# A recurrence and a mixture of experts in one kernel: TensorE's products of a step in another order

## The chip, the cores and the metric

The kernel runs on one core of a Trainium2 chip. The metric is the time of one execution on the device, in microseconds (us); the median of several runs counts. The profile comes from one more execution of the same kernel.

## The reference

```python
def _attn_ref(r, k, v, w, u):                       # B, H, S, D = 4, 8, 768, 48
    for t in range(S):
        kt, vt, rt = (k[:, :, t], v[:, :, t], r[:, :, t])
        cur = np.einsum('bhd,bhe->bhde', u[None] * kt, vt)
        y[:, :, t] = np.einsum('bhd,bhde->bhe', rt, state + cur)
        state = w[None, :, :, None] * state + np.einsum('bhd,bhe->bhde', kt, vt)
    return y

def _moe_ref(x, w_skip, w_gate, w1, w2):            # 3072 tokens of 384, 8 experts, F = 1024
    do_compute = x @ w_skip > 0
    xc = x[do_compute]
    logits = xc @ w_gate
    e_idx = np.argmax(logits, axis=1)
    gate_w = softmax(logits)[np.arange(len(xc)), e_idx]
    for e in range(E):
        h = np.maximum(xc[mask] @ w1[e], 0.0)       # mask: e_idx == e
        y[mask] = gate_w[mask, None] * (h @ w2[e])
    out[do_compute] = xc + y
```

The output of the recurrence, with the heads side by side, is the x of the experts.

## The kernel before

The recurrence is cut into chunks of 64 positions. One step handles one chunk of two batches and all heads; there are 24 steps (n = 0 to 23), 12 for each pair of batches. What a step puts on TensorE, by the function that does it:

- `scores(n+1)` (L496): products of the decayed r and k of the next chunk, 48 rows by 64 columns of the array each, four side by side, into `ps_p`. VectorE then writes them under a causal mask and on the diagonal into `am` (`mask_scores`, L508 and L509).
- `within(n)` (L550), the masked products: `am` of this chunk times v, all 128 rows by 64 columns, into `ps_y`.
- `turn_x(n-1)` (L619) and `turn_k(n+1)` (L482), the turns: transposes of the last chunk's output and of the next chunk's k, the whole array. ScalarE copies the results to `x4` (L623) and `kt` (L484).
- `state(n)` (L520), the state products: `kt` times v, 128 rows by 48 columns, added into `ps_s`. In three steps of four ScalarE then copies the state to `sblk` (`keep_state`, L538); in every fourth (n = 3, 7, 15, 19) VectorE first scales it in place (L531) and the copy comes after `across`.
- `across(n)` (L566), the carried products: r times the state in `sblk`, 48 rows by 64 columns, added onto the masked products in `ps_y`. ScalarE copies the sum out (`xt`, L579).

The last step of a pair of batches (n = 11, 23) has no state products, the first (n = 0, 12) no carried ones, and there is nothing to turn for k at n = 10 and 22.

The experts' choice runs beside this. After every fourth step `gate_four` (L636) computes the logits of four chunks, 128 rows by 32 columns, into `ps_t`; ScalarE copies them (L645), and `gate_back` (L650) turns them back. `route`, a generator, does the choice for groups of 8, 8, 4 and 4 chunks in small VectorE instructions; each `tick` or `step_route(kind)` in the loop lets it go on to its next yield of that kind. In it, `tri` and `ones` products count ranks (L732 to L742), and the list products (L841, L804) write which token goes where.

Everything is recorded by hand in the order of the code: each engine executes its instructions in that order, and waits only on semaphores of what it reads or overwrites. `behind(mm, name)` adds such a wait by hand: the first carried product waits for `turned_x[n-1]`, ScalarE's copy of the turn (L575). Products of the first expert fill the last two steps and what follows; the experts' loop comes after.

Each engine's instructions that precede VectorE's scaling in a step matter too: `prep_r(n+3)` (L446) on VectorE, after which ScalarE and GpSimd make the bonus part (L464, L456), the two mask instructions, and one tick of `route`.

## Time and profile before

| | |
|---|---|
| median of 3 runs | 271.28 us (269.43 to 272.10) |
| profiled execution, its own time | 266.43 us |
| its span, first to last instruction | 264.6 us |
| TensorE busy | 251.7 us (95%) |
| VectorE, ScalarE, GpSimd busy | 170.6, 139.4, 110.8 us |
| granted TensorE clock, mean | 0.994 |

The profiled execution was 1.8% shorter than the median of the runs, and its time is 1.8 us more than its span. The recurrence takes the first 113 us of the span, the experts the rest. TensorE's busy share says little by itself, since the ends of its matmuls are modelled; where the text needs the length of a stage it takes the distance between the starts of two stages.

### The profile page before, as it was taken

To read this page: it belongs to the slowest core of one execution; us is meant where nothing else is said; L and a number is where in the kernel's file an instruction comes from. 1 tells how busy PE (TensorE), PEld (TensorE's weight loads), DVE (VectorE), ACT (ScalarE), POOL (GpSimd) and SP (SyncE) were. 2 spreads that over 40 slices of the span, in tenths; PEclk is the share of its full clock that TensorE was granted. 3 is DMA by queue.
4 is the path that set the end of the run, shared out by engine and by line. 5 is a ranking of instruction groups with operands and counts; after the bars stand their busy time and mean duration, and the time that the engine had idled before them with its cause. 6 is when DMAs were issued, how large, how long until landed. Compare 5 with 4: busy or idle time off the path is not lost.

```text
span 264.6 us, 8597 instructions
## 1 busy us (share of the span) xinstructions
PE 251.7 (95%) x3579; PEld 225.5 (85%) x3581; DVE 170.6 (64%) x382; ACT 139.4 (53%) x315; POOL 110.8 (42%) x128
## 2 busy tenths in 40 slices
PE   7799998989999999999999999999999999999990
PEld 2578887778888888877789999999999999999990
DVE  7768555568664877737865967948659477494300
ACT  2566565656766756444773916637258174491200
POOL 8579554474765655501778151220310403105011
PEclk9999999999999999999999999999999999999997
DMA  6998699988997888496399979185291670101000
GB/s 159 245 254 257 196 257 245 274 216 242 254 265 215 246 250 266 103 345 203 108 305 285 330 215 386 54 296 231 57 398 60 223 301 18 30 0 35 11 32 24
DMA packets 20864, 52.21 MB, mean 197 GB/s; under 512 B 3556, under 2 KB 10224, under 8 KB 20816
## 3 DMA queue, kind: packets, MB, share of 16 engines
q1 hardware_dynamic: 18240, 46.42, 58.2%
q0 software_dynamic: 2048, 5.14, 6.2%
q8 instruction: 30, 0.49, 0.8%
q14 instruction: 18, 0.15, 0.2%
q10 hardware_dynamic: 528, 0.02, 0.1%
HBM read 43.77 MB, written 8.36 MB: 197 GB/s over the span
## 4 chain that ended last, share of the span: by engine, by line
PE 85%; DMA 7%; DVE 2%; issue 1%; ACT 1%; SPq 1%; POOL 0%; POOLq 0%; DVEq 0%
PE ps_p L178 11%; PE ps_y L178 11%; PE ps_l L168 11%; PE ps_p L496 8%; PE ps_y L550 7%; PE ps_s L520 6%; PE ps_p L168 5%; PE ps_x L168 5%; PE ps_y L566 5%; DMA dm<-in_dm_dram 4%; PE ps_t L619 4%; PE ps_l L482 3%; DMA raw<-in_w_dram 2%; PE ps_t L636 2%; PE ps_y L233 2%
## 5 line engine op out<-in xcount | busy, mean ns | idle before, releaser
L187 POOL DMA_INDIRECT out_dram<-xg,sid x16 | 23.7, 1478 | 89.8 <-DVE xg L183 79.8
L129 DVE TENSOR_TENSOR wlo<-raw,whi 128x512 fp32r<-128x512 f32 x84 | 54.0, 685 | 2.1 <-ACT whi L124 2.0
L124 ACT CAST whi<-raw 128x512 fp32r<-128x512 f32 x96 | 54.7, 626 | 0.0
L446 DVE TENSOR_TENSOR rd<-dm,w_d 112x512 f32<-112x512 f32 x24 | 17.7, 740 | 17.9 <-PE ps_y L566 15.6
L168 PE MATMUL ps_l<-x,whi 128*128 128x232 f32 x168 | 28.9, 274 | 0.0
L469 POOL TENSOR_TENSOR kd<-dm,w_d 112x512 f32<-112x512 f32 x22 | 28.1, 1278 | 1.0 <-DVE rd L446 1.0
L496 PE MATMUL ps_p<-rd,kd 48*64 48x128 f32 x768 | 26.4, 273 | 1.5 <-issue 0.8
L138 POOL DMA_INDIRECT xg<-out_dram,gid x16 | 19.3, 1204 | 19.7 <-DMA raw<-in_w_dram 13.4
L456 POOL TENSOR_TENSOR rd<-rd,uw 112x256 f32<-112x256 f32 x21 | 12.9, 615 | 33.1 <-DVE rd L446 23.3
L168 PEld LDWEIGHTS ps_l<-x,whi 128*128 128x128 f32 x168 | 25.5, 192 | 0.0
L464 ACT ACTIVATE rd<-rd,uw 112x128 f32<-112x128 f32 x52 | 18.0, 396 | 11.2 <-DVE rd L446 10.8
L496 PEld LDWEIGHTS ps_p<-rd,kd 48*64 48x64 f32 x768 | 20.9, 133 | 3.3 <-issue 1.4
L168 PE MATMUL ps_l<-x,wlo 128*128 128x232 f32 x84 | 23.2, 276 | 0.0
L172 ACT ACTIVATE hh<-ps_p 128x464 fp32r<-128x464 f32 x7 | 3.9, 559 | 33.1 <-PE ps_p L168 33.1
L550 PE MATMUL ps_y<-vkv,am 128*64 128x96 f32 x384 | 21.1, 252 | 0.1
L508 DVE COPY_PREDICATED am<-below,ps_p 128x512 f32<-128x512 int8 x24 | 17.7, 736 | 4.7 <-PE ps_p L496 4.3
L550 PEld LDWEIGHTS ps_y<-vkv,am 128*64 128x64 f32 x384 | 16.6, 136 | 4.2 <-issue 2.9
L520 PE MATMUL ps_s<-vkv,kt 128*48 128x96 f32 x352 | 19.4, 251 | 0.8 <-issue 0.8
L623 ACT COPY x<-ps_t 128x384 f32<-128x384 f32 x23 | 11.0, 478 | 16.0 <-PE ps_t L619 15.9
L178 PE MATMUL ps_p<-whi,hh 128*128 128x384 f32 x56 | 19.4, 347 | 0.0
L178 PE MATMUL ps_y<-whi,hh 128*104 128x384 f32 x56 | 18.9, 338 | 0.0
L178 PE MATMUL ps_p<-whi,hl 128*128 128x384 f32 x56 | 18.9, 337 | 0.0
(239 smaller groups left out, 591.2 us busy)
## 6 DMA issues: line engine op xcount, KB each, us to landing
raw<-in_w_dram SPq DMA_DIRECT2D x16, 768.0 KB, 7.9
dm<-in_dm_dram SPq DMA_DIRECT2D x24, 448.0 KB, 5.3
raw<-in_w_dram SPq DMA_DIRECT2D x24, 256.0 KB, 5.5
raw<-in_w_dram SPq DMA_DIRECT2D x12, 512.0 KB, 5.5
out_dram<-xt SPq DMA_DIRECT2D x26, 192.0 KB, 4.3
vkv<-in_tok_dram SPq DMA_DIRECT2D x22, 192.0 KB, 4.5
vkv<-in_tok_dram SPq DMA_DIRECT2D x4, 96.0 KB, 6.5
out_dram<-xt SPq DMA_DIRECT2D x4, 96.0 KB, 4.3
```

The costliest lines, as they stand in the source:

```text
L124: nc.scalar.copy(wsp[e][0][:, s], raw[e][:, s])
L129: eng.tensor_tensor(lo[:, s], raw[e][:, s], hi[:, s].bitcast(F32), ALU.subtract)
L138: ins = nc.gpsimd.indirect_dma_start(out=xg[:m], out_offset=None, in_=out[:rows], in_offset=bass.IndirectOffsetOnAxis(ap=gid[:m, q : q + 1 ...
L168: nc.tensor.matmul(ph, w1[a][:, c, fs], x[:, c, b, :], start=(k == 0), stop=(k == 3 * NCC - 1))
L178: nc.tensor.matmul(py, a, b[:, f, :], start=(k == 0), stop=(k == 3 * NFC - 1))
L187: ins = nc.gpsimd.indirect_dma_start(out=out, out_offset=bass.IndirectOffsetOnAxis(ap=sid[:m, q : q + 1], axis=0), in_=xs.pop(q)[:m], in_o ...
L446: ins = nc.vector.tensor_tensor(rd[:, :, :, 0], d, w_d[:, n % NSUB, 0][:, None].to_broadcast([DR, NB, NHP, C]), ALU.mult)
L464: nc.scalar.activation(rd[:, :, hp, 1], rd[:, :, hp, 0], AF.Copy, scale=uw[:, hp : hp + 1])
L469: ins = (eng or nc.gpsimd).tensor_tensor(kds[n].rearrange("p b h c -> p b (h c)"), d, w_d[:, n % NSUB, 1].rearrange("p h c -> p (h c)")[:, ...
L496: mm = nc.tensor.matmul(ps_p[g * C : (g + 1) * C, a, j * P : (j + 1) * P], kd[h, b, hp, :], rd[h, b, hp].rearrange("p s c -> p (s c)"), st ...
L520: nc.tensor.matmul(s[a * C : a * C + D, j * 2 * D : (j + 1) * 2 * D], kt[:, j, a, :], v[:, j, a], start=i == 0 and j == 0, stop=True, skip ...
L550: nc.tensor.matmul(ps_y[b * C : (b + 1) * C, a, jj * 2 * D : (jj + 1) * 2 * D], am[n % 2][:, a, j * C : (j + 1) * C], v[:, j, a], start=jj ...
```

## The change

Inside a step, the state products go directly behind the masked ones, and both turns behind them; in every fourth step (where logits are due) the turn of x stays ahead, because the logits need it, and the turn of k goes behind the logits, followed by the turn back of the logits. The list products of kinds 2 and 4 go there too, ahead of the carried products instead of behind them. The first carried product waits for whatever read the state just before: ScalarE's copy of it, or VectorE's scaling in every fourth step (in steps without state products it waits for the copy of the turn, as before). `x4` becomes one tile for the whole kernel, and the factors of the lists, `vl`, have one buffer instead of two.

```diff
             if sub == NSUB - 1:
                 q = s.rearrange("p (b h e) -> p b h e", b=NB, h=NHP)
                 for b in range(NB):
-                    nc.vector.tensor_tensor(
+                    ins = nc.vector.tensor_tensor(
                         q[:, b], q[:, b], wh_sb.unsqueeze(2).to_broadcast([DR, NHP, D]), ALU.mult
                     )
             else:
-                keep_state(n)
+                ins = keep_state(n)
+            read_state[n] = ins.ins.name
...
                         if hp == 0 and (a, b) == FOUR[0]:
-                            behind(mm, turned_x[n - 1])
+                            behind(mm, read_state.get(n, turned_x[n - 1]))
...
-                if n % 4 == 0:
-                    x4[n // 4] = wk.tile([P, NCC, 4, P], F32, tag="x4", name=f"x4{n}", bufs=1)
-                done = nc.scalar.copy(x4[n // 4][:, :, n % 4, :], pt[:, :DM].rearrange("p (c q) -> p c q", c=NCC))
+                done = nc.scalar.copy(x4[:, :, n % 4, :], pt[:, :DM].rearrange("p (c q) -> p c q", c=NCC))
...
-            vl = small("vl", F32R, NV3 * NSL)
+            vl = small("vl", F32R, NV3 * NSL, 1)
...
             if n + 1 < NT:
                 mask_scores(n + 1)
                 tick()
+            four = n % 4 == 0 and n > 0
+            if four:
+                turn_x(n - 1)
             if n > 0:
-                turn_x(n - 1)
-                if (n + 1) % NSTEP < NSTEP - 1 and n + 1 < NT:
-                    turn_k(n + 1)
                 state(n)
             if four:
                 gate_four(n // 4 - 1)
+            elif n > 0:
+                turn_x(n - 1)
+            if 0 < n < NT - 1 and (n + 1) % NSTEP < NSTEP - 1:
+                turn_k(n + 1)
+            if four:
+                gate_back(n // 4 - 1)
+            if n < NT - 1:
+                step_route(2)
+                if n < NT - 3:
+                    step_route(4)
             warm(FILL.get(n, 0))
             tick(0 if n < HURRY else 6)
...
-            if n != NSTEP:
-                step_route(2)
-            if n == NSTEP + 1:
-                gate_back(n // 4 - 1)
-            if four and n != NSTEP:
-                gate_back(n // 4 - 1)
-            if n < NT - 3 or n == NT - 1:
+            if n == NT - 1:
                 step_route(4)
-            if n == NT - 1:
                 step_route(4)
```

`across(n)` and `mask_scores(n+1)` stand where they stood. Two lines were added above `within`, so that L550, L566 and L619 of before are L552, L568 and L621 after.

TensorE's order in steps 15 and 16 (step 16 is one with logits), from the scores of step 15 to those of step 17, before:

```order
L496 MATMUL ps_p<-rd_1323,kd_1328 64x128 x16
L550 MATMUL ps_y<-vkv_124,am_150 64x96 x8
L619 MATMUL ps_t<-ident,xt_1469 128x128 x3
L482 MATMUL ps_l<-ident,kd_1328 128x112 x4
L520 MATMUL ps_s<-vkv_124,kt_1442 48x96 x8
L566 MATMUL ps_y<-sblk_198,rd_1243 64x48 x16
L496 MATMUL ps_p<-rd_1414,kd_1419 64x128 x16
L550 MATMUL ps_y<-vkv_125,am_149 64x96 x8
L619 MATMUL ps_t<-ident,xt_1469 128x128 x3
L482 MATMUL ps_l<-ident,kd_1419 128x112 x4
L520 MATMUL ps_s<-vkv_125,kt_1515 48x96 x8
L636 MATMUL ps_t<-x_1346,wg_sb 32x128 x12
```

The rows that follow are L566, L650 and the next L496. The same stretch on TensorE after the change:

```order
L496 MATMUL ps_p<-rd_1333,kd_1338 64x128 x16
L552 MATMUL ps_y<-vkv_124,am_150 64x96 x8
L520 MATMUL ps_s<-vkv_124,kt_1448 48x96 x8
L621 MATMUL ps_t<-ident,xt_1466 128x128 x3
L482 MATMUL ps_l<-ident,kd_1338 128x112 x4
L568 MATMUL ps_y<-sblk_199,rd_1241 64x48 x16
L496 MATMUL ps_p<-rd_1411,kd_1416 64x128 x16
L552 MATMUL ps_y<-vkv_125,am_149 64x96 x8
L621 MATMUL ps_t<-ident,xt_1466 128x128 x3
L520 MATMUL ps_s<-vkv_125,kt_1522 48x96 x8
L636 MATMUL ps_t<-x_197,wg_sb 32x128 x12
L482 MATMUL ps_l<-ident,kd_1416 128x112 x4
```

In step 15 the state products (L520) moved from behind the turns to directly behind the masked ones; in step 16 only the turn of k (L482) moved, and L650 now follows it and precedes the carried products.

TensorE at step 19, where the wait of the first carried product changes, with the engines that a row waits for (49 belongs to the semaphore's name); before:

```order
L550 MATMUL ps_y<-vkv_123,am_150 64x96 [waits Activation_49]
L550 MATMUL ps_y<-vkv_123,am_150 64x96 x7
L619 MATMUL ps_t<-ident,xt_1804 128x128 x3
L482 MATMUL ps_l<-ident,kd_1662 128x112 x4
L520 MATMUL ps_s<-vkv_123,kt_1777 48x96 x8
L566 MATMUL ps_y<-sblk_198,rd_1567 64x48 [waits Activation_49]
```

And TensorE at step 19 after:

```order
L552 MATMUL ps_y<-vkv_123,am_150 64x96 [waits Activation_49]
L552 MATMUL ps_y<-vkv_123,am_150 64x96 x7
L520 MATMUL ps_s<-vkv_123,kt_1782 48x96 x8
L621 MATMUL ps_t<-ident,xt_1800 128x128 x3
L482 MATMUL ps_l<-ident,kd_1659 128x112 x4
L568 MATMUL ps_y<-sblk_199,rd_1564 64x48 [waits DVE_49]
```

The carried products of this step now wait for VectorE (DVE) and no longer for ScalarE (Activation). The same row changes in the same way at steps 3, 7 and 15.

VectorE's order changes in one place, at steps 12 and 13, where the list products of the first route moved a step forward: their reader (`lists`, L844) and L847 went ahead of `prep_r(16)`, L446. VectorE there after the change:

```order
L834 TENSOR_TENSOR vl_1264<-ps_x,id_193 128x8x16
L834 TENSOR_TENSOR vl_1264<-ps_x,gh_1143 128x8x16
L834 TENSOR_TENSOR vl_1264<-ps_x,gl_1144 128x8x16
L844 COPY lists<-ps_x 128x48
L847 TENSOR_SCALAR over<-r_1145 128x8
L446 TENSOR_TENSOR rd_1333<-dm_1085,w_d 112x8x64
L508 COPY_PREDICATED am_149<-below,ps_p 128x512
L509 COPY_PREDICATED am_149<-eye,ps_p 128x512
```

Before, L844 and L847 stood behind that L509. ScalarE executes the same copies, with the copy of the state ahead of those of the turns; the orders of GpSimd and of the DMA queue of SyncE are the same.

## Rows read from the trace of the kernel before

**Rows 1.** Windows, steps 2 to 22: length; busy (count) by engine; clock; DMA share; GB/s.

```profile
20.20:112.70 92.50, 90.53 (x2245) 76.38 (x2242) 60.98 (x151) 57.70 (x143) 55.29 (x64) 1.00 0.85 235
```

**Rows 2.** Timeline of TensorE, step 15: start, length, line, tiles, shape, count.

```profile
77.13 1.07 PE L496 MATMUL ps_p<-rd,kd 48*64 48x128 f32 x32
78.13 0.88 PE L550 MATMUL ps_y<-vkv,am 128*64 128x96 f32 x16
78.94 0.55 PE L619 MATMUL ps_t<-ident,xt 128*128 128x128 f32 x3
79.32 0.55 PE L482 MATMUL ps_l<-ident,kd 112*128 112x112 f32 x4
79.80 0.87 PE L520 MATMUL ps_s<-vkv,kt 128*48 128x96 f32 x16
80.60 0.68 PE L566 MATMUL ps_y<-sblk,rd 48*64 48x48 f32 x32
81.10 0.30 PE L496 MATMUL ps_p<-rd,kd 48*64 48x128 f32 x4
```

**Rows 3.** The same timeline cut off shortly after the first state products.

```profile
79.80 0.37 PE L520 MATMUL ps_s<-vkv,kt 128*48 128x96 f32 x4
```

**Rows 4.** Timeline of TensorE, the end of step 16 and the start of 17.

```profile
85.36 0.68 PE L566 MATMUL ps_y<-sblk,rd 48*64 48x48 f32 x32
85.97 0.33 PE L650 MATMUL ps_t<-ident,l 128*128 128x128 f32 x1
86.23 1.10 PE L496 MATMUL ps_p<-rd,kd 48*64 48x128 f32 x32
```

**Rows 5.** Timeline of TensorE's weight loads, step 15; in brackets idle time before.

```profile
78.12 0.69 PEld L550 LDWEIGHTS ps_y<-vkv,am 128*64 128x64 f32 x16 [0.17 <-issue]
79.21 0.45 PEld L482 LDWEIGHTS ps_l<-ident,kd 112*128 112x128 f32 x4
```

**Rows 6.** Timeline of VectorE, step 15.

```profile
79.04 0.74 DVE L509 COPY_PREDICATED am<-eye,ps_p 128x512 f32<-128x512 int8 x1
80.78 0.77 DVE L531 TENSOR_TENSOR ps_s<-ps_s,pw 112x192 f32<-112x192 f32 x2 [1.01 <-PE ps_s L520]
```

**Rows 7.** Timeline of ScalarE, step 16.

```profile
84.74 0.48 ACT L538 COPY sblk<-ps_s 112x384 f32<-112x384 f32 x1 [0.33 <-PE ps_s L520]
85.50 0.27 ACT L645 COPY l<-ps_t 128x128 f32<-128x128 f32 x1 [0.28 <-PE ps_t L636]
```

**Rows 8.** Timelines of TensorE and of VectorE, step 19 (L834: step 20).

```profile
94.64 1.10 PE L496 MATMUL ps_p<-rd,kd 48*64 48x128 f32 x32
98.15 0.27 PE L566 MATMUL ps_y<-sblk,rd 48*64 48x48 f32 x4
...
94.75 0.23 DVE L760 TENSOR_TENSOR rkp<-ps_x,oh 128x64 f32<-128x64 f32 x1 [1.42 <-PE ps_x L742]
98.33 0.77 DVE L531 TENSOR_TENSOR ps_s<-ps_s,pw 112x192 f32<-112x192 f32 x2
103.15 0.27 DVE L834 TENSOR_TENSOR vl<-ps_x,gl 128x128 fp32r<-128x128 f32 x1
```

**Rows 9.** Timeline of TensorE, step 10, which turns no k.

```profile
57.09 0.88 PE L550 MATMUL ps_y<-vkv,am 128*64 128x96 f32 x16
59.17 0.68 PE L566 MATMUL ps_y<-sblk,rd 48*64 48x48 f32 x32
```

**Rows 10.** Timelines of VectorE and TensorE, end of step 12.

```profile
67.90 0.28 DVE L834 TENSOR_TENSOR vl<-ps_x,gl 128x128 fp32r<-128x128 f32 x1
...
67.83 1.10 PE L496 MATMUL ps_p<-rd,kd 48*64 48x128 f32 x32
```

**Rows 11.** Timelines of ScalarE and of TensorE, step 1.

```profile
18.20 0.46 ACT L623 COPY x<-ps_t 128x384 f32<-128x384 f32 x1
...
18.70 0.51 PE L566 MATMUL ps_y<-sblk,rd 48*64 48x48 f32 x20 [0.47 <-ACT x L623]
```

**Rows 12.** The chain of waits, behind the recurrence.

```profile
119.10 5.57 DMA raw<-in_w_dram
```

More of the change, by code (lines that the diff above doesn't have):

```diff
@@ L439, in setup_routes @@
             )
-        rds, kds, kts = {}, {}, {}
+        rds, kds, kts, read_state = {}, {}, {}, {}
         def prep_r(n):
@@ L534, in state @@
             else:
-                keep_state(n)
+                ins = keep_state(n)
+            read_state[n] = ins.ins.name
         def keep_state(n):
-            nc.scalar.copy(sblk[(n + 1) % 2], ps_s[:DR, : NB * NHP * D])
+            return nc.scalar.copy(sblk[(n + 1) % 2], ps_s[:DR, : NB * NHP * D])
         xts, pair = {}, [None]
+        x4 = tab.tile([P, NCC, 4, P], F32, name="x4")
         sblk = [tab.tile([DR, NB * NHP * D], F32, name=f"sblk{j}") for j in range(2)]
@@ L628, in turn_x @@
             gts[n] = (pt, xT)
-        x4, l4, turned_x = {}, {}, {}
+        l4, turned_x = {}, {}
         def gate_four(g):
-            x, m = x4.pop(g), min(4, GATED - 4 * g)
+            m = min(4, GATED - 4 * g)
             for c in range(NCC):
@@ L638, in gate_four @@
                         wg_sb[:, c, :],
-                        x[:, c, j, :],
+                        x4[:, c, j, :],
                         start=(c == 0),
@@ L796, in route @@
                     nc.vector.tensor_copy(ohp, oh)
-                vl = small("vl", F32R, NV3 * E)
+                vl = small("vl", F32R, NV3 * E, 1)
                 for q, val in enumerate(vals):
@@ L939, in tile_wkv_moe @@
         for n in range(NT):
-            four = n % 4 == 0 and n > 0
             if 0 < n < NT - 4 and n % 2 == 0:
```

## The prediction

> **What bounds the kernel now.** I read the windows first. [...] Then the timeline of TensorE: step 15 is a plain step, and the distances between the starts of its stages are 1.00 for the scores, 0.81 masked products, 0.38 turn of x, 0.48 turn of k, 0.80 state products, 0.50 carried products, 3.97 us in all [rows 2]. Nothing in it waits for another engine. What it loses stands between the stages: the state products come in pairs, and with 4 of the 16 issued the stage ends at 0.37 instead of 0.87 [rows 2, 3], so six pairs take 0.50, 0.083 each. Eight pairs would take 0.66; the stage takes 0.80. I call the missing 0.14 a seam: the array goes from one tile shape to another, the first weight load stands in the open and the first product is slow. The weight loads show it: the first load of the masked products starts at 78.12 after 0.17 us idle, with its product at 78.13, while between the turns of x and of k, which have 128 and 112 rows, the load runs ahead, 79.21 against 79.32 [rows 2, 5]. A second way to the same price: carried products followed by scores, both 48 by 64, take 0.50 [rows 2]; with the turn back of the logits between them it is 0.87 [rows 4]. Of the extra 0.37 a turn among turns would take a quarter of the 0.48 for four, 0.12; two seams share the other 0.25, 0.13 each. I take 0.14.
>
> **The change, part by part.** No product is added or removed; what changes is the number of seams and what a stage waits for.
>
> State products behind the masked ones. A plain step has four seams now (scores, masked, turns, state, carried, and no seam from carried to scores) and three afterwards, if 64 and 48 columns on 128 rows are one shape. I say they are, because from 128 to 112 rows the load runs ahead [rows 2, 5]; then a plain step takes 3.83 us. The bounds of the gain are 0 and 0.14. Plain steps in which nothing else decides are 2, 5, 6, 9, 13, 14, 17, 18 and 21: nine times 0.14, 1.26 us. In step 1 the carried products wait for ScalarE, whose bonus of step 4 stands ahead of either copy [rows 11]; the wait stays and the seam is not seen.
>
> The carried products' wait. Count from the start S of a step's scores. The state stage now begins at S + 1.00 + 0.72 and the turns at S + 2.47; the carried products are due at S + 3.33 (2.47 + 0.38 + 0.48). The state products end 0.07 after the next stage starts (79.80 + 0.87 against 80.60 [rows 2]), at S + 2.54, and their reader starts 0.11 later (80.78 against 80.67 [rows 2, 6]), at S + 2.65.
> With ScalarE as reader the copy takes 0.48 [rows 7], and with 0.04 to TensorE (a copy's end at 18.66, TensorE's start at 18.70 [rows 11]) it releases at S + 3.17. That is covered by the two turns, with 0.16 to spare. In steps 10 and 22, which turn no k, the cover is gone: due at S + 2.95 (the turn of x with its seam is 0.48), released at 3.17, while before the carried products began at S + 3.08 (1.00 + 59.17 - 57.09 [rows 9]). Two steps lose 0.1 each, 0.2 us.
> With VectorE as reader (steps 3, 7, 15, 19) the scaling takes 0.77 [rows 6]. In step 15 the masks end at 79.78, S + 2.65, just as the state is ready; scaling would end at 3.42, and with the handovers the release is at S + 3.50 instead of 3.33. Before, they began at S + 3.47 [rows 2]. So steps 3, 7 and 15 lose 0.03 each, 0.1 us.
> Step 19 is another matter. There VectorE has the second route's instructions in its queue. It takes up the ranks at 94.75, after an idle wait for the rank products, and is occupied without a break until the scaling, which runs from 98.33 to 99.10 [rows 8]. The scaling stays behind a tick of the route. So the backlog, not the state, sets its start, and an earlier state product cannot move it. The carried products began at 98.15 before, with nobody waiting for the scaling but a later copy; now they begin at 99.14. Loss 1.0 us, and no seam gained. What follows is not pushed further: the lists' factors end at 103.42 [rows 8], some 0.3 later when `prep_r(23)` waits for those carried products, and the list products of step 20 are due only at about 104.1.
>
> Steps with logits (4, 8, 16, 20). The turn back and, at 20, the list products stop being an island between carried products and scores, which had two seams; the turn of k and they form a stage of their own behind the logits, one seam. Net one seam, 0.14, four times: 0.56. The turn back needs ScalarE's copy of the logits, which ended 0.41 after the logits' stage (85.77 against 85.36 [rows 4, 7]); the turn of k ahead of it takes 0.48, so it is about covered; at most 0.05 is lost each time. I count 0.5.
>
> List products of the first route, now at step 12. They spare one seam too, but they come 1.4 us before their old neighbours: TensorE reaches them at about 68.03 (the scores began at 67.83 [rows 10]; the slow first turn and the turn back come on top), and VectorE's factors are ready at 68.18 + 0.05 [rows 10]. Wait 0.2, seam 0.14: a loss of 0.06. VectorE's own queue then waits for these products about 1 us before `prep_r(16)`; ScalarE's and GpSimd's bonus and the k of step 16 are late by as much, but its scores are two steps off. No price.
>
> The one tile `x4` and the single buffer of `vl` cost nothing: `x4` had one buffer before, and the second route's factors are written some 35 us after the first's were read [rows 8, 10]. The DMA queue's order is the same; at 85% [rows 1] a step that is 3.5% shorter still fits. Behind the recurrence the chain of waits leaves TensorE: ScalarE's copies of the last outputs, the issue, a weight transfer of 5.57 us [rows 12]. All of it starts from the end of the recurrence, so what is gained there moves on to the end.
>
> **Sum:** 1.26 + 0.5 - 0.06 - 0.1 - 0.2 - 1.0 = 0.4 us less. The profiled execution's 266.43 us becomes 266.0. The median of the runs is 4.9 us above that execution, which I cannot place; I carry the difference over: 271.28 - 0.4 = 270.9 us.
>
> **The rivals.** First, step 19 is not held: VectorE's backlog is shorter in the changed order, by its waits on other engines moving, and the scaling ends before the turns do. Then 1.0 + 0.14 comes back, 1.5 us faster in all, 269.7. Against it speaks that VectorE's work there has no idle time that could go.
> Second, slower: the seam between masked and state products stays, because 48 columns are another shape than 64. Then the nine plain steps gain nothing, and in steps 3, 7, 10, 15 and 22 the reader starts 0.14 later than I said: 0.4 - 1.26 - 0.7, 1.6 us slower, 272.8. It decides from the point where the first load of the state products cannot run ahead under the last masked products. Against it: inside the masked stage loads do run ahead, 16 of them in 0.69 us without idle time though all use the same 128 rows [rows 5].
> [...]
> Third, no net effect: another queue takes up the gain. Should the transfers of r and k, at their 85%, be late once the steps are shorter, TensorE waits for what it saved, and the losses of steps 10 and 19 are hidden by the same waits: 271.3.
>
> **How the numbers follow.** The forecast has 0.55, the first rival 0.15, the second 0.15, the third 0.15. All lie within 1% of 271.28 us (2.7 us), which is about what a measurement of this kernel can tell from no change: its three runs alone span 2.7 us. The range reaches from the first rival to the second and takes in about 1 us of the runs' own scatter below and little above, since the second rival is already the far end: 268.6 to 272.9. Scatter can carry the first rival over the bound on one side and the second on the other: faster by over 1% 0.14, within 1% 0.75, slower by over 1% 0.11.
>
> **What would show it.** In the changed kernel's timeline a plain step of 3.83 us, with the state products starting 0.72 after the masked ones and their first load ahead of their first product (right), or 0.81 after and the load in the open (second rival). At step 19 the carried products with an idle time of about 1.1 us, released by VectorE's scaling, L531. Idle times of 0.1 to 0.2 before the carried products in steps 3, 7, 10, 15 and 22 and before the list products of step 12. The forecast is wrong if TensorE waits anywhere else, above all for `rd`, `kd` or `vkv`, or if the stretch behind the recurrence changes its length by more than 0.5 us.

## The result and the profile after

| | before | after |
|---|---|---|
| median of 20 runs | 267.98 us (266.05 to 273.03) | 268.94 us (267.21 to 271.18) |
| profiled execution, its own time | 266.43 us | 267.21 us |
| its span | 264.6 us | 265.4 us |
| recurrence, first to last masked products | 100.42 us | 99.95 us |

The ratio after to before is 1.0052, with an interval of 1.0028 to 1.0076: by this ratio the changed kernel is half a per cent slower, some 1.4 us, where 0.4 us less was forecast. The ratio compares the executions within 1.5% of each kernel's fastest; six of before's 20 lie above that, and over all 20 the means are 268.86 and 268.95 us.

The plain steps look as predicted. Timeline of TensorE, kernel after, step 2, a plain one (start, length, line, tiles, shape, count):

```profile
19.12 1.07 PE L496 MATMUL ps_p<-rd,kd 48*64 48x128 f32 x32
20.12 0.88 PE L552 MATMUL ps_y<-vkv,am 128*64 128x96 f32 x16
20.83 0.83 PE L520 MATMUL ps_s<-vkv,kt 128*48 128x96 f32 x16
21.59 0.55 PE L621 MATMUL ps_t<-ident,xt 128*128 128x128 f32 x3
21.97 0.55 PE L482 MATMUL ps_l<-ident,kd 112*128 112x112 f32 x4
22.45 0.68 PE L568 MATMUL ps_y<-sblk,rd 48*64 48x48 f32 x32
22.95 1.07 PE L496 MATMUL ps_p<-rd,kd 48*64 48x128 f32 x32
```

From scores to scores it is 22.95 - 19.12 = 3.83 us, where step 15 of before took 3.97 [rows 2], and the state products start 0.71 after the masked ones. The weight loads of that step agree (timeline of TensorE's weight loads):

```profile
20.75 0.71 PEld L520 LDWEIGHTS ps_s<-vkv,kt 128*48 128x48 f32 x16
```

The first load of the state products starts at 20.75, 0.08 us ahead of their first product and before the last masked product has started. The seam between them is gone.

Timelines of TensorE and of VectorE, kernel after, step 19:

```profile
95.80 0.55 PE L482 MATMUL ps_l<-ident,kd 112*128 112x112 f32 x4
97.40 0.68 PE L568 MATMUL ps_y<-sblk,rd 48*64 48x48 f32 x32 [1.05 <-DVE ps_s L531]
...
96.50 0.17 DVE L784 TENSOR_TENSOR gl<-ps_x,gh 128x8 fp32r<-128x8 f32 x1
96.58 0.76 DVE L531 TENSOR_TENSOR ps_s<-ps_s,pw 112x192 f32<-112x192 f32 x2
```

The carried products stand idle 1.05 us for the scaling, as the forecast said; before, they started at 98.15 without a wait [rows 8]. The view of waits of TensorE, first of before, then of after (us in total, times, longest):

```profile
PE ps_s L520 <- issue: 0.8, 1, 0.8
PE ps_p L496 <- issue: 0.8, 1, 0.8
...
PE ps_y L566 <- issue: 0.2, 1, 0.2
```

```profile
PE ps_y L568 <- DVE ps_s L531: 1.2, 2, 1.1
PE ps_p L496 <- issue: 1.2, 2, 1.1
PE ps_l L168 <- issue: 1.1, 1, 1.1
PE ps_y L568 <- ACT sblk L539: 0.9, 3, 0.6
```

Beside the predicted waits for VectorE (L531) and ScalarE (L539), both kernels have waits on "issue": TensorE stood still, and the profile shows nothing that it waited for. Before has 1.8 us of them in three pieces, after 2.3. One of after's is no part of the recurrence (timeline of TensorE, expert 1, kernel after):

```profile
144.55 0.27 PE L168 MATMUL ps_x<-x,wlo 128*128 128x232 f32 x1
145.95 0.49 PE L168 MATMUL ps_l<-x,whi 128*128 128x232 f32 x2 [1.13 <-issue]
```

This gap adds 1.1 us behind the recurrence, where the trace of before has none. So in this pair the recurrence was 0.47 us shorter, and the stretch behind it 1.41 us longer (from the last masked products to the start of TensorE's last product: 146.18 us for 144.77). Windows of the kernel after, steps 2 to 22 (to be held against rows 1), and 36 to 56 us (length; columns as in rows 1):

```profile
20.12:112.14 92.02, 88.88 (x2245) 75.76 (x2242) 61.42 (x150) 57.14 (x143) 55.30 (x66) 1.00 0.85 237
36.00:56.00 20.00, 18.85 (x499) 16.06 (x493) 12.56 (x26) 12.96 (x34) 12.06 (x13) 1.00 1.02 285
```

### The profile page after: what moved, and what is told of

Same layout as the page of the kernel before. It is cut to its first block, busy times and chain, and to the rows that moved or that the text cites. A ratio compares the mean times of both kernels' runs of the same rounds, so it can differ in the third digit from the quotient of the medians.

```text
span 265.4 us, 8593 instructions
## 1 busy us (share of the span) xinstructions
PE 250.7 (94%) x3581; PEld 225.0 (85%) x3581; DVE 171.1 (64%) x382; ACT 138.8 (52%) x315; POOL 109.2 (41%) x128
## 4 chain that ended last, share of the span: by engine, by line
PE 79%; DMA 7%; DVE 6%; issue 2%; ACT 1%; SPq 1%; POOL 0%; POOLq 0%; DVEq 0%; ACTq 0%
PE ps_p L178 11%; PE ps_y L178 11%; PE ps_l L168 11%; PE ps_p L496 7%; PE ps_y L552 6%; PE ps_p L168 5%; PE ps_y L568 5%; PE ps_x L168 5%; PE ps_s L520 4%; DMA dm<-in_dm_dram 4%; PE ps_t L621 3%; PE ps_l L482 2%; DMA raw<-in_w_dram 2%; PE ps_t L636 2%; DVE rd L446 2%
## 5 line engine op out<-in xcount | busy, mean ns | idle before, releaser
L187 POOL DMA_INDIRECT out_dram<-xg,sid x16 | 22.5, 1408 | 92.8 <-DVE xg L183 89.1
L446 DVE TENSOR_TENSOR rd<-dm,w_d 112x512 f32<-112x512 f32 x24 | 18.1, 755 | 20.4 <-PE ps_y L568 15.0
L496 PE MATMUL ps_p<-rd,kd 48*64 48x128 f32 x768 | 26.7, 272 | 1.7 <-issue 1.2
L496 PEld LDWEIGHTS ps_p<-rd,kd 48*64 48x64 f32 x768 | 21.2, 133 | 3.0 <-issue 1.9
L172 ACT ACTIVATE hh<-ps_p 128x464 fp32r<-128x464 f32 x7 | 3.9, 560 | 34.0 <-PE ps_p L168 28.3
L552 PE MATMUL ps_y<-vkv,am 128*64 128x96 f32 x384 | 21.4, 253 | 0.1
L552 PEld LDWEIGHTS ps_y<-vkv,am 128*64 128x64 f32 x384 | 16.8, 136 | 4.3 <-issue 3.6
L178 PE MATMUL ps_y<-wlo,hh 128*104 128x384 f32 x56 | 18.9, 337 | 0.0
L178 PE MATMUL ps_y<-whi,hl 128*104 128x384 f32 x56 | 18.9, 337 | 0.0
```

Source lines behind the costliest of these rows:

```text
L178: nc.tensor.matmul(py, a, b[:, f, :], start=(k == 0), stop=(k == 3 * NFC - 1))
L187: ins = nc.gpsimd.indirect_dma_start(out=out, out_offset=bass.IndirectOffsetOnAxis(ap=sid[:m, q : q + 1], axis=0), in_=xs.pop(q)[:m], in_o ...
L446: ins = nc.vector.tensor_tensor(rd[:, :, :, 0], d, w_d[:, n % NSUB, 0][:, None].to_broadcast([DR, NB, NHP, C]), ALU.mult)
L496: mm = nc.tensor.matmul(ps_p[g * C : (g + 1) * C, a, j * P : (j + 1) * P], kd[h, b, hp, :], rd[h, b, hp].rearrange("p s c -> p (s c)"), st ...
L552: nc.tensor.matmul(ps_y[b * C : (b + 1) * C, a, jj * 2 * D : (jj + 1) * 2 * D], am[n % 2][:, a, j * C : (j + 1) * C], v[:, j, a], start=jj ...
```

## The experiments

Theory A: the order gains what was forecast, and TensorE loses it in gaps in which it has no instructions to execute. Theory B, the rival: the waits on the state's reader cost more than one trace shows. Theory C: the new places of the tiles. Theory E came up on the way: the place where TensorE's blocks of instructions end decides. All ratios are to the kernel before on the same chip; "recurrence" is the distance from the first to the last masked products in the run's trace, and "gaps" are the distances from start to start of the two instructions of TensorE around a block end, less what is usual there (mostly 0.05 us). (The idle time in brackets is shorter, since a product's end is modelled.)

### The changed kernel again

> The changed kernel once more, unchanged, for a second interval and a second trace. In the first comparison it was 0.52% slower (interval 0.28 to 0.76%), while its trace shows the recurrence 0.5 us shorter and a gap of TensorE of about 1.1 us behind it. Theory A (the order gains its 0.5 us, and TensorE loses it in gaps in which it waits for nothing but its own instructions): the recurrence is again 0.4 to 0.6 us shorter than in the trace of before, the ratio again 1.002 to 1.008, and the gaps without a releaser add up to more than before's 1.8 us. Theory B (the waits on the state's reader cost more in most executions than in the one that was profiled): the recurrence in this trace is 0.5 us or more longer than in the first trace of this kernel, with longer waits at the carried products. Chance of the first trace: ratio within 0.2% of 1.000.

1.0109 (1.0050 to 1.0168), from 6 runs only, three of 267.67 to 268.83 us and three of 271.82 to 272.39. Recurrence 100.36 us, which is 0.4 longer than the first time: the carried products of step 8 stood for 1.46 us on "issue". The waits on the state's reader were the same to 0.02 us. Theory B's longer waits are not there. Theory A's numbers failed too: the recurrence is 0.06 us shorter than in the trace of before, not 0.4 to 0.6, and the ratio lies above its range.

### VectorE's tick behind the scaling

```diff
                 mask_scores(n + 1)
-                tick()
...
                 state(n)
+            if n + 1 < NT:
+                tick()
```

> The changed kernel, with VectorE's tick of the route behind the scaling of the state and no longer ahead of it; this moves four small instructions behind the scaling in step 19 and nothing else on any engine. Theory B: the carried products of step 19 wait 0.65 us less (four instructions, from 95.90 to 96.58 in the changed kernel's trace), so 0.4 us instead of 1.1 us, and the time falls by 0.6 to 0.7 us, ratio to before 1.002 to 1.003. Theory A: the wait gets shorter by as much, but the time need not follow; ratio 1.002 to 1.008.

1.0027 (0.9991 to 1.0062). Step 19 took 4.27 us instead of 4.96, as both theories said. The recurrence was 100.86 us all the same, since two gaps on "issue" took 1.31 and 1.20 us. The ratio fits either theory.

### The state products alone

```diff
+            read_state[n] = ins.ins.name
...
+                            behind(mm, read_state.get(n, turned_x[n - 1]))
...
             if n > 0:
+                if not four:
+                    state(n)
                 turn_x(n - 1)
...
-                state(n)
+                if four:
+                    state(n)
```

> The kernel before with the state products directly behind the masked ones and the carried products waiting for the state's reader, in the steps without logits alone; the steps with logits, the turn back, the list products and the buffers stay as they were. By the terms of the forecast: nine plain steps save 0.14 each (1.26), steps 3, 7, 15, 10, 22 and 19 lose 1.3, so no difference: 0.9985 to 1.002. If the loss of 0.5% comes from this part (theory B): 1.004 to 1.008. If it comes from the moves around the logits and lists, or from the buffers: within 0.1% of 1.000.

1.0078 (1.0038 to 1.0118), slower, as theory B said. But the trace shows what its span of 270.1 us was spent on (an execution of 271.80 us; the median was 270.48). Windows of this kernel around 50 us (columns as above):

```profile
46.00:50.00 4.00, 2.80 (x66) 2.20 (x65) 0.65 (x1) 1.66 (x4) 0.91 (x1) 1.00 1.03 299
50.00:54.00 4.00, 3.01 (x48) 2.37 (x50) 1.21 (x4) 1.69 (x5) 1.47 (x2) 0.56 0.97 254
54.00:57.00 3.00, 3.00 (x34) 2.75 (x35) 2.29 (x6) 0.17 (x1) 1.60 (x2) 0.50 0.49 156
57.00:61.00 4.00, 4.00 (x105) 3.56 (x104) 2.20 (x6) 2.95 (x9) 1.60 (x2) 0.96 0.19 43
```

TensorE stood on "issue" for 2.19 us up to 50.99, and behind that the granted clock was low until about 57 us, 0.56 from 50 to 54 us and 0.50 from 54 to 57: the recurrence of 104.61 us has 3.6 us of gaps and the low clock in it. Its waits for L531 are 1.2 us, those of the changed kernel. What the other executions were spent on is not shown.

### The buffers alone

```diff
+        x4 = tab.tile([P, NCC, 4, P], F32, name="x4")
...
-            vl = small("vl", F32R, NV3 * NSL)
+            vl = small("vl", F32R, NV3 * NSL, 1)
```

> The kernel before with x4 as one tile of the whole kernel and the lists' factors with one buffer, and no instruction of any engine moved. Theory C (the new places of the tiles cost time, by which transfers and reads meet in the memory): 1.004 to 1.008. Theories A and B: within 0.15% of 1.000.

1.0015 (0.9976 to 1.0054): no effect that can be told from none. Theory C's 1.004 to 1.008 is not met, but the interval reaches 1.0054, so a part of the 0.5% is not ruled out. Its trace too has gaps on "issue", of 1.3 and 1.1 us.

### The kernel before again

> The kernel before, unchanged, run as an experiment: how far a kernel's ratio to itself can lie from 1.000, and a second trace of it. All theories: ratio 0.997 to 1.003. In the trace: theory A (TensorE waits for its own instructions, whose blocks stand behind the data in DMA engines that are 97 to 100% busy from 36 to 56 us) expects gaps without a releaser at the same instruction numbers as in the other traces, about 1984 and 2240, with other lengths, and the late signal at 145 us, which five traces of other kernels show and the first trace of this one doesn't, to be here or not by chance. If the gap at 145 us is missing again, it belongs to what the kernels differ in, and 1.4 us of the difference are there.

1.0019 (0.9982 to 1.0056). In this trace the gap at 145 us is there (1.07 us, at 146.40), and the stretch behind the recurrence takes 146.10 us, as in after. So it does not belong to the change. Its recurrence was 100.25 us. The gaps on "issue" are not at the instruction numbers that theory A named: TensorE had issued 1619, 1746 and 2383 products by then (727, 982 and 1109 in the first trace), and from 36 to 56 us there is no gap, though the DMA engines were busy for 1.02 of that stretch.

### Fewer transfers

```diff
-        nc.scalar.copy(wsp[e][0][:, s], raw[e][:, s])
+        r = s if e else slice(0, WCOLS // NPC)
+        nc.scalar.copy(wsp[e][0][:, s], raw[e][:, r])
...
-            if n in RAW0:
+            if n == RAW0[0]:
                 load_expert(0, RAW0.index(n), 12)
```

For the lighter pair also, in `load_v`:

```diff
+            if n >= 8:
+                return
```

> The kernel before with 11 of the 12 transfers of the first expert's weights during the recurrence left out (its split reads the first piece twelve times, so the output of that expert is not the reference's); no instruction of TensorE, VectorE, ScalarE or GpSimd moved. 2.9 MB of about 22 MB less in the recurrence. Theory A: the gaps at the block numbers shrink below 0.5 us in all, the recurrence falls from 100.4 us to 98.5 to 99.5 us, and the ratio is 0.985 to 0.996. Theory B: the transfers don't matter for TensorE, ratio within 0.3% of 1.000.

> The changed kernel with the same eleven transfers left out. Theory A: with the gaps gone, the terms of the forecast are left: the recurrence is 0.2 to 0.6 us shorter than that of the light kernel before, and the light pair's ratio, after to before, is 0.997 to 1.000, where the full pair's is 1.005 to 1.011. Theory B: the light pair differs as the full one does, 1.004 to 1.010, and the recurrence after is the longer one.

> The kernel before with eleven transfers of the first expert's weights and the eight pairs of transfers of v for steps 8 to 23 left out (old data are used in their place); no instruction of the computing engines moved. 6 MB of about 22 MB less in the recurrence. Theory A: no gap without a releaser over 0.3 us is left in the recurrence, which is 97.5 to 97.9 us from the first masked products to the last; most executions lie within 0.5 us of each other, at 264.5 to 265.3 us.

> The changed kernel with the same transfers left out. With every step taken at its shortest in the traces so far, the recurrence is 97.67 us before and 97.71 after: what the plain steps save (0.14 each), steps 19, 3, 10, 21 and 22 lose. Theory A with this sum: no gap without a releaser over 0.3 us, a recurrence of 97.5 to 97.9 us, and the lighter pair equal within 0.2%. If the forecast's sum of 0.4 us stands: 0.998 to 0.999 of the lighter kernel before. Theory B (the new order itself costs more than a trace shows): 1.004 to 1.010 of it.

| | ratio | interval | median | recurrence | gaps at block ends |
|---|---|---|---|---|---|
| before, light | 0.9908 | 0.9869 to 0.9947 | 265.33 us | 97.88 us | none |
| after, light | 0.9924 | 0.9892 to 0.9956 | 265.73 us | 100.23 us | 1.6 us |
| before, lighter | 0.9971 | 0.9932 to 1.0009 | 265.99 us | 97.88 us | none |
| after, lighter | 0.9917 | 0.9882 to 0.9951 | 265.82 us | 97.81 us | none |

Windows from 36 to 56 us, where the gaps were: the kernel before from 24 to 70 us in three pieces, and the two lighter kernels.

```profile
24.00:36.00 12.00, 12.00 (x295) 9.94 (x287) 6.96 (x11) 7.05 (x19) 7.84 (x14) 1.00 0.80 214
36.00:56.00 20.00, 18.49 (x478) 15.38 (x470) 11.24 (x23) 12.39 (x32) 9.85 (x10) 1.00 0.97 263
56.00:70.00 14.00, 13.54 (x332) 11.32 (x333) 11.30 (x31) 8.83 (x22) 9.04 (x10) 1.00 0.84 237
```

```profile
36.00:56.00 20.00, 20.00 (x527) 16.93 (x525) 12.65 (x27) 13.64 (x35) 11.35 (x12) 1.00 0.62 177
```

```profile
36.00:56.00 20.00, 19.92 (x536) 17.03 (x528) 13.16 (x27) 13.59 (x35) 11.76 (x13) 1.00 0.66 179
```

The DMA engines, busy for 0.97 of that stretch before and 1.02 after, fall to 0.62 and 0.66 in the lighter pair, and with that every gap is gone. This fits theory A, by which the gaps come with busy DMA engines, though such a stretch does not always have one: at 0.85, in the light kernel before, there is none either. What it said of the order is not confirmed: with no gap left, the two recurrences differ by 0.07 us. For the light pair it failed, since the changed kernel kept a gap of 1.4 us. It also failed for the scatter: the executions of the lighter kernel before lie between 264.26 and 268.57 us and not within 0.5 us of each other; whether the longer ones had gaps is not known. Theory B is not confirmed either: in the lighter pair the changed kernel is not the slower one.

### Where the gaps stand

```diff
-        def warm(k, to=ps_l):
+        def warm(k, to=ps_l, w=512):
...
-        warm(NWARM, ps_t)
+        warm(NWARM + 32, ps_t, 160)
```

> The changed kernel with the 15 products of 512 columns that open TensorE's program cut into 47 of 160 columns: about the same work, and 64 more instructions ahead of everything else, so that blocks of 256 instructions end 64 instructions earlier in the recurrence, by about 1.2 us. Theory A: the gaps without a releaser stand again at instruction numbers that leave the same remainder by 256 (194), which is now another place of the code: in the earlier traces the gap of about 1.5 us at 49 us is inside the carried products, here it is 64 instructions ahead of it. If the gaps are tied to the place in the code (a tile, a transfer of data), they stay at the same products. The time: 1.000 to 1.010 either way.

1.0001 (0.9961 to 1.0041). Timeline of TensorE: two sides of the gap in the kernel after, then of one in this kernel.

```profile
52.72 0.61 PE L496 MATMUL ps_p<-rd,kd 48*64 48x128 f32 x10
54.40 0.77 PE L496 MATMUL ps_p<-rd,kd 48*64 48x128 f32 x19 [1.07 <-issue]
```

```profile
62.72 0.46 PE L552 MATMUL ps_y<-vkv,am 128*64 128x96 f32 x5
64.19 0.71 PE L552 MATMUL ps_y<-vkv,am 128*64 128x96 f32 x11 [1.01 <-issue]
```

Windows from the start to the middle of a gap count the products and weight loads that TensorE had issued by then: three gaps of before, one of after, two of this kernel.

```profile
0.00:39.60 39.60, 35.90 (x727) 26.99 (x730) 27.21 (x60) 21.27 (x53) 27.08 (x56) 1.00 0.87 228
0.00:50.20 50.20, 45.68 (x982) 35.19 (x984) 32.19 (x68) 27.42 (x68) 32.00 (x61) 1.00 0.89 235
0.00:55.60 55.60, 50.82 (x1109) 39.35 (x1111) 35.89 (x79) 30.78 (x77) 35.08 (x64) 1.00 0.90 235
```

```profile
0.00:53.60 53.60, 49.78 (x1112) 38.77 (x1112) 36.49 (x79) 30.88 (x79) 35.10 (x64) 1.00 0.90 241
```

```profile
0.00:57.60 57.60, 53.35 (x1239) 45.23 (x1240) 38.69 (x84) 33.17 (x84) 37.76 (x67) 1.00 0.89 239
0.00:63.30 63.30, 58.23 (x1366) 49.23 (x1366) 43.42 (x99) 35.94 (x91) 39.61 (x69) 1.00 0.90 240
```

727, 982, 1109 or 1112, 1239 and 1366 products: the distances are 255, 127 to 130, 127 and 127, always about 127 products with as many loads, or twice that. In this kernel, with 32 products more at its start, the gap is inside the masked products, not the scores. So the gaps of these three kernels stand where a block of about 255 loads and products ends, whatever is computed there. With the instructions of TensorE's sequencer counted too, the three gaps of before stand behind 1471, 1983 and 2239 of its records, 512 and 256 apart. Just ahead of the gap of after, which lasts from 53.06 to 54.40 us, one packet of instructions moved (view of DMA queues, 51.6 to 53.0 us: packets, MB, share):

```profile
q1 hardware_dynamic: 142, 0.33, 102.0%
q8 instruction: 1, 0.02, 5.3%
```

That packet stands among 142 packets of data that fill the engines. It ends at 52.84 us, and the products go on 1.56 us later. The times of such packets agree with this in both traces of the pair: each of the five waits on "issue" of over 0.1 us that the two recurrences have from 20 us on ends 1.3 to 1.6 us behind the end of a packet of that queue (at 40.36, 50.37 and 56.28 us in before, where packets end at 39.08, 49.02 and 54.83; at 54.40 and 75.94 in after, where they end at 52.84 and 74.54). (The queue moves 30 of them in before's execution, 0.49 MB, about 16 KB each; TensorE's 7215 records, 7160 of them products and loads, make 28 blocks of 256.) The other 29 block ends in that time TensorE passes without such a wait, 28 of them 1.45 to 4.72 us behind the end of the packet and one, at 45.07 us in before, 0.85 us behind. So a gap reads as TensorE waiting for its next instructions; the one end that was passed after 0.85 us does not fit, and why is open.

### Other places of the block ends

> The changed kernel with VectorE's tick behind the scaling (as in the second experiment) and steps 3, 10 and 22 in the old order. By the shortest steps of the traces this saves 0.68 in step 19, 0.11 in step 3 and 0.09 each in 10 and 22, 0.97 us against the changed kernel and 0.93 us against the kernel before, which is 0.35%. Theory A: what it saves comes out at the end only as far as the gaps at the block ends stay what they were: 0.996 to 1.003 of the kernel before. Theory B: 0.996 to 0.998, below the changed kernel by 0.4% or more in any case.

> The kernel of the run beside it with the opening products cut as in the experiment on block ends (64 more instructions ahead). Theory A: the same recurrence but for the gaps, which stand at other products; which of the two is faster can't be said, difference up to 1%. If the gaps don't depend on the block ends: the same time within 0.3%.

> The kernel before with the 15 opening products of 512 columns cut into 47 of 160 columns, so that its blocks of 256 instructions end 64 instructions earlier. Theory A: the gaps move to other products and stay 1 to 4 us in all; the changed kernel moved by as much was 1.0001 of before, and this one lies within 0.5% of it: 0.996 to 1.005. Theory E (the position of the block ends decides which order is the faster): one of the two shifted kernels is 0.5% or more from the other.

> The changed kernel with 79 opening products of 96 columns, 128 more instructions than the changed kernel has. Theory A: gaps of 1 to 4 us in all, at instruction numbers with the remainder 194, half a block from those of the changed kernel; 0.998 to 1.008. Theory E: a time that differs from the changed kernel's and from that shifted by 64 by 0.5% or more.

> The kernel before with 128 more instructions in its opening (79 products of 96 columns for 15 of 512). Theory E (the place of the block ends decides): a time between 0.993 and 1.006 of before that the trace's gaps account for: its recurrence is 97.7 us, its shortest, plus the sum of the gaps at the block ends, within 0.4 us. If the shift by 64 helped for another reason, such as the longer opening itself: 0.993 again, with gaps of 2 us or more.

> The changed kernel with VectorE's tick behind the scaling, steps 3, 10 and 22 in the old order, and the same 128 instructions more. By the shortest steps its recurrence is 96.8 us, 0.9 less than before's, plus the gaps. Theory E: between 0.991 and 1.004; its recurrence is 96.8 us plus the sum of its gaps, within 0.4 us. If the order decides at a common place of the block ends: 0.35% less than the run beside it, 0.25 to 0.45%.

The order of the first of these, against the changed kernel:

```diff
+                            behind(mm, turned_x[n - 1] if n in (3, 10, 22) else read_state.get(n, turned_x[n - 1]))
...
-                tick()
...
+            first_x = four or n in (3, 10, 22)
+            if first_x:
                 turn_x(n - 1)
+            if n == 3:
+                turn_k(n + 1)
             if n > 0:
                 state(n)
+            if n + 1 < NT:
+                tick()
...
-            elif n > 0:
+            elif n > 0 and not first_x:
                 turn_x(n - 1)
-            if 0 < n < NT - 1 and (n + 1) % NSTEP < NSTEP - 1:
+            if 0 < n < NT - 1 and n != 3 and (n + 1) % NSTEP < NSTEP - 1:
                 turn_k(n + 1)
```

| instructions more | before | after | after, three steps back |
|---|---|---|---|
| 0 | 1.0019 (0.9982 to 1.0056) | 1.0052 (1.0028 to 1.0076) | 1.0030 (0.9990 to 1.0070) |
| 64 | 0.9937 (0.9905 to 0.9969) | 1.0001 (0.9961 to 1.0041) | 1.0023 (0.9983 to 1.0062) |
| 128 | 0.9992 (0.9955 to 1.0029) | 0.9975 (0.9939 to 1.0012) | 0.9932 (0.9900 to 0.9965) |
| gaps in the trace | 2.0, 0.7, 2.4 us | 1.7, 2.5, 2.3 us | 2.9, 2.3, 1.8 us |
| recurrence | 100.25, 98.43, 100.92 us | 99.95, 100.98, 100.80 us | 100.26, 100.02, 99.09 us |

Same order, other block ends: the ratios of before span 0.8%, those of after 0.8%, those of the third 1%. The runs of a column are from two or three chips, so these spans can hold differences of chips too. What one chip shows is this: the 64 instructions alone made the kernel before 0.63% faster (0.9937), and they left the third order where it was (1.0030 and 1.0023). Theory B's 0.996 to 0.998 for the third order without more instructions is missed. The kernel before shifted by 64 has two short gaps left, 0.39 us ahead of the masked products and about 0.35 us inside the logits, whose stage takes 1.15 us for 0.79 (timeline of TensorE, 36 to 56 us):

```profile
37.75 0.88 PE L550 MATMUL ps_y<-vkv,am 128*64 128x96 f32 x16 [0.32 <-issue]
48.16 1.21 PE L636 MATMUL ps_t<-x,wg_sb 128*32 128x128 f32 x24
```

The same kernel shifted by 128 has these in that stretch, and the third order at 128 has its longest much later:

```profile
42.26 0.45 PE L496 MATMUL ps_p<-rd,kd 48*64 48x128 f32 x7 [0.33 <-issue]
49.37 0.44 PE L619 MATMUL ps_t<-ident,xt 128*128 128x128 f32 x2 [1.62 <-issue]
```

```profile
88.97 0.31 PE L568 MATMUL ps_y<-sblk,rd 48*64 48x48 f32 x2 [1.23 <-issue]
```

```profile
0.00:88.00 88.00, 82.78 (x2001) 70.39 (x2003) 58.57 (x132) 53.10 (x133) 56.94 (x86) 1.00 0.91 244
```

That last one stands behind 2001 products, seven times 127 behind after's 1112: a block end again. Theory A's 0.996 to 1.005 for before at 64 is missed. Theory E's numbers are met for the two kernels shifted by 64 (0.64% apart, on two chips) and half met for after at 128, which is 0.8% from after and only 0.3% from after at 64. Of the two fastest kernels one has the old order (at 64) and one the new with three steps back (at 128); both are 0.6 to 0.7% faster than before, and so faster than both kernels of the study. At 128, on the same chip, the third order is ahead of the old one, medians 264.73 and 266.06 us, by more than the 0.35% that its steps save; at 64 its ratio is the higher one, on another chip. So neither order is shown to lead at every place. The sum that was expected of each recurrence, its shortest steps plus its gaps within 0.4 us, is missed by 0.8 us (97.7 + 2.4 against 100.92) and 0.5 us (96.8 + 1.8 against 99.09): the longer opening makes step 1 late, by 0.7 and 0.5 us.

### Weights later

```diff
-WSPLIT = (6, 8, 9, 11, 12, 13, 15, 16, 17, 19, 20, 21)
+WSPLIT = (6, 8, 9, 12, 13, 14, 15, 16, 17, 19, 20, 21)
...
-RAW0 = (3, 5, 6, 8, 9, 11, 12, 14, 15, 17, 18, 19)
+RAW0 = (3, 5, 6, 10, 11, 12, 13, 14, 15, 17, 18, 19)
```

> The kernel before with four transfers of the first expert's weights issued one to two steps later (steps 10, 11, 12 and 13 for 8, 9, 11 and 12) and their splits on ScalarE and GpSimd one step later, so that half a megabyte less stands in the DMA queue from 45 to 55 us. Theory A: the gaps near instructions 1986 and 2242 (49 and 54 us) shrink below 0.5 us together, the recurrence is 0.5 to 2 us shorter than in the traces of before, and the ratio is 0.992 to 0.998; what is saved there can be lost again at 65 to 80 us, where the transfers now are. Theory B: no difference, 0.998 to 1.003.

> The same four transfers later, in the changed kernel with VectorE's tick behind the scaling and steps 3, 10 and 22 in the old order. By the shortest steps its recurrence is 0.9 us shorter than before's. Theory A: with the gaps smaller, up to 0.9 us less than the run beside it: ratio 0.989 to 0.997, faster than both kernels. If the order's gain goes into gaps whatever their place: the same as the run beside it within 0.2%.

0.9967 (0.9931 to 1.0002) and 0.9969 (0.9935 to 1.0003): equal, and not clearly faster than before. The gap at 49 us did not shrink (1.35 and 1.37 us idle), though in before's order the DMA share from 44 to 56 us fell from 0.98 to 0.83. Gaps of 2.47 us (before's order, 84.57) and 1.47 us (78.72) stand at block ends that had 0 to 1.1 us idle in the other traces. The first of the two traces is of an execution of 271.66 us, 5.8 above that kernel's median, so its long gap need not be usual. Theory A's numbers for this pair failed.

## Why the prediction was wrong

Inside the steps its mechanisms were right, but two terms of its sum were mis-sized, and its claim that the queues could follow was wrong. The lighter pair has no gaps, so its steps can be held against the terms one by one (after minus before, us from masked products to masked products):

| term | forecast | lighter pair |
|---|---|---|
| plain steps 2, 5, 6, 9, 14, 17, 18 | -0.98 | -0.97 |
| step 21 | -0.14 | +0.13 |
| steps 12 and 13, the lists | -0.08 | -0.06 |
| steps 4, 8, 16, 20, the logits | -0.5 | -0.27 |
| steps 3, 7, 15 | +0.1 | +0.13 |
| steps 10 and 22 | +0.2 | +0.18 |
| step 19 | +1.0 | +0.97 |
| sum | -0.4 | +0.1 |

Step 1, whose 0.18 us in the kernel before is in no other trace of it, is left out.

- **The seam** was sized to 0.01 us, and steps 19, 10 and 22 to 0.03: the waits for L531 and for L539 came where they were said to come. Two other sums are right by luck. Step 3 lost 0.11 us and steps 7 and 15 lost 0.01 each, where 0.03 each was forecast; and the list products of step 12, said to wait 0.2 us, start 0.07 late here and without a wait in the first trace of after.

```profile
PE ps_y L572 <- DVE ps_s L535: 1.2, 2, 1.0
PE ps_y L572 <- ACT sblk L543: 0.9, 3, 0.6
```

- **The logits' term was mis-sized.** A step saves 0.07, not 0.13. Stage by stage in step 16 of this pair, from start to start, the carried products take 0.50 us for 0.61, the scores 1.00 for 1.03 and the turn of k 0.46 for 0.48. But the turn of x, now followed by the state products and not by another turn, takes 0.48 for 0.38. The forecast counted one seam less at 0.14; the seams that went and the one that came are not of one size.
- **Step 21** has a pause inside its masked products here (0.85 us up to the state products for 0.72), and the state products take 0.89 us for 0.76. Three of the last traces (after at 128, three steps back at 128 and with weights later) don't have it: the step takes 4.05 us there for 4.18 in before, the forecast's -0.13. Why is open.
- So the order by itself costs 0.1 us in this pair, and saves 0.15 us where step 21 goes as in those three traces; neither is the 0.4 us of the forecast. The 0.47 us by which the first trace's recurrence was shorter looks like the forecast and is not its proof: the gaps in the two executions differ by more (2.4 us before, 1.7 after).
- **Two steps failed.** In the sum it is the logits' term (0.27 us saved for 0.5) and step 21 (0.13 lost for 0.14 saved): together they take away the gain of 0.4 us. The other step is "at 85% [rows 1] a step that is 3.5% shorter still fits". The 85% is a mean over 92 us. From 36 to 56 us the share is 0.97, and in both kernels TensorE stands still there until 1.3 to 1.6 us after a packet of instructions has come through among the data. The rows had a sign of it: 2 of the 92.5 us [rows 1] were not busy, and the prediction went on from one step in which nothing waits. The third rival had another queue take up the gain, but through r and k; by the times of the packets it is the instructions, and they don't only take up, they can go either way. Of the prediction's signs against itself one came, the stretch behind the recurrence longer by 1.41 us; but the second trace of before has it as well.
- **The size, +0.5%,** is not traced to one gap, since the runs that set the median are not profiled. What is shown: gaps of 1.7 to 4.7 us stood in all but one of the traces with all transfers, of either order (0.7 us in that one); without them the changed order is not the slower one; and on one chip 64 more instructions ahead, with the order untouched, moved the kernel before by 0.63%, more than the change did. What is not shown is that the new order's block ends are worse in each execution. A kernel against itself gave 1.0019 with an interval up to 1.0056, and over all 20 executions the means of the two kernels are 0.03% apart, so part of the 0.5% may be scatter. The cause of the 0.5% stays open.
- The first rival (step 19 not held) and the second (the seam stays) are refuted by the timeline after. The 4.9 us between median and profiled execution was no property of the kernel: with 20 runs it was 1.6. That the median of 268.94 us lies inside the range of the forecast is luck for the same reason: the base of 271.28 us, from three runs, was 3.3 us above the median of 20, and the change went the other way.

## What to carry to other kernels

Read the DMA share by stretches, not as a mean, and count the waits on "issue" before calling an engine unhindered: here TensorE went through a block of 256 instructions in 4.85 us (from 45.07 to 49.92 us in before), and the wait behind that block ended 1.35 us after the end of a packet of instructions. So look up when an engine's program arrives, and not its data alone. Where such gaps are as large as the change, compare each order at several places of the block ends, and against itself, before a difference of half a per cent is put down to the order. A sum of small terms needs every step looked up by itself: what the logits' steps save was priced by a count of seams at one price, and was half of it.

## What was not expected of the hardware

- Gaps of TensorE at the ends of blocks of about 255 loads and products, up to 2.47 us idle (before's order with weights later); in the traces of before and after each of the five ended 1.3 to 1.6 us behind the end of a packet of instructions. Those two traces show DMA shares of 0.97 and 1.02 from 36 to 56 us; at 0.62 and 0.66 (the lighter pair) there was none. A high share does not always bring one: there was none at 0.85 (the light kernel before), and none in that stretch at 1.02 (the second trace of before).
- Behind some of them the granted clock fell to 0.50: for 6.8 us behind 2.19 and behind 2.47 us idle, and for 3.4 us, in two other traces, behind 1.33 and 1.37 us, but not behind 1.35, 1.46, 1.47 and 1.62.
- A weight load of 48 columns ran ahead under products of 64 columns, all on 128 rows: in step 2 of after it started 0.08 us ahead of its product, with 0.71 us from masked to state products.
- The gap of 1.1 us at 145 us goes with a late read of the tile: ScalarE reads `ps_l` (L172) at 144.66 in after, 2.1 us after its last product was issued, and at 143.38 in before, 0.3 us after it. It was in the first trace of after and the second of before, and in none of the traces of the last six kernels, of either order. Its cause is open.
